# Linear attention and a mixer MLP on one core: loads over two queues, and the key sum z spread by crossbar turns

## The chip, the cores and the metric

The kernel runs on one core of a Trainium2 chip. The metric is device time in microseconds (us) of one execution; lower is better. A core has TensorE (PE, matmuls into PSUM), VectorE (DVE), ScalarE (ACT), GpSimd (POOL) and SyncE (SP, here only a queue that issues DMAs). ScalarE and GpSimd can issue DMAs as well.

## The reference

Two branches read the same `x` (2048 tokens of 640 channels, bf16) and are mixed by a gate per token. `B_x` is not used.

```python
qkv = x @ wqkv                                   # 640 -> 3*640, 32 heads of 20
pq, pk = phi(q), phi(k)                          # phi(t) = t+1 if t>0 else exp(t), + 1e-6
kv  = einsum("bhsd,bhse->bhde", pk, v)
z   = einsum("bhsd->bhd", pk)                    # sum of pk over all tokens: 640 numbers
num = einsum("bhqd,bhde->bhqe", pq, kv)
den = einsum("bhqd,bhd->bhq", pq, z) + 1e-6
a = (num / den) @ wo
h = gelu(layernorm(x) @ w1)                      # then four groups of channels are shifted by 1 or 2 tokens
x1 = x + shifted(h) @ w2
b = x1 + gelu(layernorm(x1) @ w3) @ w4
out = g * a + (1 - g) * b                        # g = sigmoid(sum(x * gate_w))
```

## The kernel before

The tokens lie in 16 tiles of 128 (tokens on the partitions), in four chunks of 512. Everything stays in SBUF. The stages overlap, but TensorE runs through them in about this order:

1. Head. TensorE first runs matmuls of ones (`warmup`, L854), then turns the first three x tiles itself (`t_x`, L763: five 128x128 transposes into one PSUM bank, then a VectorE copy into `xT`). `stream` (L873) with the order written out in `q_three` (L896) multiplies these tiles by the five 128-row blocks of wq, block by block as they land; `k_two` (L905) does the same for two k tiles. Each of these 25 steps is one matmul of 512 and one of 128 or 130 columns.
2. q and k tiles 2 to 15 (`k_tile`, `q_tile`). The x tiles from 3 on are turned by the DMA crossbar (`x_turn`, a transposing DMA on SP's queue). `phi` takes each result through ScalarE (Exp) and VectorE.
3. G = x-transposed times pk, in five row blocks (`gt_step`, L812) and a tail. ScalarE copies each finished block from PSUM into `GT`; the last block is item `("g", 4)`. On VectorE, 15 additions (`z_add`, L822) sum the 16 pk tiles to `zsum` (128 partitions of 640 partial sums).
4. `kvt_group` (L953; its matmuls are L969) multiplies wv by `GT`; VectorE masks the result into `Lt` (`lt_evac`), and two `m_step`s (L998) multiply it by wo into `M_sb`.
5. Around stage 4, `w1_group` (L1041) and `w2_tile` (L1049) of the MLP. They read `xnT`, the turned normalized x: GpSimd normalizes a tile into `xn` (a ring of three slots, `normalize`, L843), and SP issues its crossbar turn into `xnT` (`t_xn`, L849). ScalarE writes w1's results as `hsT`.
6. `zb_group` (L1025): two matmuls with a matrix of ones sum `zsum` over the partitions and spread the result over all of them; VectorE casts it to `zb`. `qn_sum` (L1086) multiplies each q tile by `zb` for the denominators.
7. w3, w4, the attention output (`a_tile`) and the mix.

Each engine runs its own instruction list in order. The order of the lists is not written out by hand but planned when the program is built: every piece of work is an item in a stream with dependencies and lags, and `_Items.run` always takes the item that a cost model expects to be ready first. An item puts all its instructions at the end of their engines' lists at once. The semaphore waits are derived from the buffers that instructions share. Loads go out in the order of the code:

```python
    for c in range(1, NCH):
        t0 = 5 if c == 1 else 4 * c
        dma_in(x_tok[:, t0:4 * c + 4, :], ...)
        for t in range(4 * c, 4 * c + 4):
            x_turn(t)
```

After the sixteen xn turns SP issues the loads of w3 and w4.

Of the kernel before, what the change touches and what calls it, by code (L numbers as in the profile page):

```python
# [6 lines left out]
F32 = mybir.dt.float32  # L7
ACTF = mybir.ActivationFunctionType
ALU = mybir.AluOpType
# [407 lines left out]
def _build(nc, A_x, A_wqkv, A_wo, B_w1, B_w2, B_w3, B_w4, gate_w, out, dbg=None, stop=None):  # L417
# [45 lines left out]
    def psb(b, n0, n1):  # L463
        return ps[:, b, :].bitcast(BF16)[:, n0:n1]
# [21 lines left out]
    M_sb = pa.alloc("M_sb", [128, KD, D], BF16)  # L486
    zb = pa.alloc("zb", [128, D], BF16)
    dnr = pa.alloc("dnr", [128, 2, 4, H], F32)
    xn = pa.alloc("xn", [128, 3, D], BF16)
    junk = pa.alloc("junk", [128, 1, D], BF16)  # L490
    qprod = pa.alloc("qprod", [128, D], F32)
# [22 lines left out]
    def bank():  # L514
        best = None
        for k_ in range(nbanks[0]):
            b = (bank_rr[0] + k_) % nbanks[0]
            if b in bank_pend or b in bank_hold:
                continue
            lk = sch.locks.get(b)  # L520
            tfree = 0.0 if lk is None else sch.ev_time.get((lk[1].sem, lk[1].val), 1e18)
            if best is None or tfree < best[0]:
                best = (tfree, b)
        bank_rr[0] = best[1] + 1
        bank_pend.add(best[1])
        return best[1]
# [4 lines left out]
    def pair():  # L531
        best = None
        for k_ in range(4):
            q_ = (bank_rr[0] // 2 + k_) % 4
            tf = 0.0
            ok = True
            for b in (2 * q_, 2 * q_ + 1):
                if b in bank_pend or b in bank_hold:
                    ok = False
                lk = sch.locks.get(b)  # L540
                if lk is not None:
                    tf = max(tf, sch.ev_time.get((lk[1].sem, lk[1].val), 1e18))
            if ok and (best is None or tf < best[0]):
                best = (tf, 2 * q_)
        b = best[1]
        bank_rr[0] = b + 2
        bank_pend.update((b, b + 1))
        return b
# [24 lines left out]
    def dve(fn, reads, writes, cost=None):  # L573
        if cost is None:
            n = nfree(writes[0])
            cost = 65.0 + n / 0.96
        return sch.op("dve", fn, reads, writes, cost=cost)
# [16 lines left out]
    def mm_group(out_ap, pairs, reads_extra=()):  # L594
        n = len(pairs)

        def fn(e, out_ap=out_ap, pairs=pairs, n=n):
            ins = None
            for i, (l, r) in enumerate(pairs):
                ins = e.matmul(out_ap, l, r, start=(i == 0), stop=(i == n - 1))  # L600
            return ins
        reads = [a for p in pairs for a in p] + list(reads_extra)
        return pe(fn, reads, [out_ap], cost=n * (max(nfree(pairs[0][1]), 24) * 0.4167 + 2.5))

    def tr_group(b, srcs):
        outs = [psb(b, 128 * i, 128 * (i + 1)) for i in range(len(srcs))]

        def fn(e, outs=outs, srcs=srcs):
            ins = None
            for o, s_ in zip(outs, srcs):  # L610
                ins = e.transpose(o, s_, ident[:])  # L611
            return ins
        return pe(fn, list(srcs) + [ident[:]], [psb(b, 0, 128 * len(srcs))], cost=len(srcs) * 56.0)
# [29 lines left out]
    def activation(out_ap, in_ap, func, scale=1.0, bias=0.0, accum=None):  # L643
        rd = [in_ap] + [a for a in (scale, bias) if not isinstance(a, (int, float))]
        wr = [out_ap] + ([accum] if accum is not None else [])
        n = nfree(out_ap)
        cost = max(150.0, 100.0 + 0.833 * n + (70.0 if in_psum(in_ap) else 0.0)) + 45.0 * (len(rd) - 1)
        if accum is not None:
            cost += 91.0
        st_ = ACT_SET.get(func)  # L650
        if st_ is not None and st_ != sch.act_func:
            cost += 1290.0
            sch.act_func = st_
        if accum is not None:
            return act(lambda e: e.activation(out_ap, in_ap, func, bias=bias, scale=scale, accum_out=accum), rd, wr, cost=cost)  # L655
        return act(lambda e: e.activation(out_ap, in_ap, func, bias=bias, scale=scale), rd, wr, cost=cost)  # L656
# [4 lines left out]
    def copy(engf, out_ap, in_ap):  # L661
        cost = None
        if engf is dve and in_ap.dtype == BF16 and out_ap.dtype == BF16:
            cost = 65.0 + nfree(out_ap) / 1.92
        return engf(lambda e: e.tensor_copy(out_ap, in_ap), [in_ap], [out_ap], cost=cost)  # L665
# [7 lines left out]
    def dma_in(out_ap, in_ap, key, **kw):  # L673
        return sch.dma("sp", out_ap, in_ap, key, **kw)

    sch.dma("act", junk[0:16, 0, 0:80].rearrange("p (k f) -> p k f", k=KD),
            A_wqkv[:, 0:16].rearrange("(k e r) f -> e r k f", k=KD, r=8)[:, 0, :, :], "touch")
    dma_in(x_tok[:, 0, :], x2[0:128, :], "x0")
    dma_in(x_tok[:, 1, :], x2[128:256, :], "x1")
    def load_wq(k):  # L680
        dma_in(wq[:, k, :], A_wqkv[128 * k:128 * (k + 1), 0:D], "wq%d" % k)

    load_wq(0)
    dma_in(x_tok[:, 2, :], x2[256:384, :], "x2")
    for k in range(1, KD):
        load_wq(k)
    for k in range(KD):
        dma_in(wkg[:, k, 0:D], A_wqkv[128 * k:128 * (k + 1), D:2 * D], "wk%d" % k)
        if k == 0:
            dma_in(x_tok[:, 3, :], x2[384:512, :], "x3")  # L690

    def x_turn(t):
        sch.dma("sp", xT[:, :, 128 * t:128 * (t + 1)], x_tok[:, t, :], "trx%d" % (t % 4), transpose=True)

    dma_in(x_tok[:, 4, :], x2[512:640, :], "x4")
    x_turn(3)
    gwr = xn[:, 1, 0:128]
    dve(lambda e: e.memset(gwr, 0.0), [], [gwr])
    sch.dma("act", xn[0:KD, 1, 0:128], gate_w.rearrange("(k p) -> k p", p=128), "gw")
    for c in range(1, NCH):  # L700
        t0 = 5 if c == 1 else 4 * c
        dma_in(x_tok[:, t0:4 * c + 4, :], x2[128 * t0:512 * (c + 1), :].rearrange("(n p) d -> p n d", p=128), "xc%d" % c)
# [54 lines left out]
        assert tags.get((buf, sl)) == what, ("stale ring slot", buf, sl, what, tags.get((buf, sl)))  # L757

    IT = _Items()
    WARM = 3200  # L760
    WARM2 = 512

    def t_x(t):  # L763
        b = bank()
        tr_group(b, [x_tok[:, t, 128 * k:128 * (k + 1)] for k in range(KD)])
        src = psb(b, 0, D).rearrange("p (k c) -> p k c", k=KD)
        dst = xT[:, :, 128 * t:128 * (t + 1)]
        if t == 2:
            mm_group(ps[:, b, 448:448 + KD], [(gwr, ident[:, 0:KD])])
        copy(dve, dst, src)  # L770
        if t == 2:
            copy(dve, wkg[:, :, D + 1:D + 2], ps[:, b, 448:448 + KD].rearrange("p (k o) -> p k o", o=1))

    def phi(b, dst, after_exp=None):
        se = slot("E", 3)
# [96 lines left out]

    def stream(order, w, n2, done):  # L873
        bs = {}
        for t, k in order:
            if k is None:
                if t is None:
                    warmup(256, 0.42)
                else:
                    t_x(t)  # L880
                continue
            if k == 0:
                bs[t] = pair()
                bank_hold.update((bs[t], bs[t] + 1))
            b = bs[t]
            l = xT[:, k, 128 * t:128 * (t + 1)]

            def fn(e, l=l, b=b, k=k):
                e.matmul(ps[:, b, 0:512], l, w[:, k, 0:512], start=(k == 0), stop=(k == KD - 1))  # L889
                return e.matmul(ps[:, b + 1, 0:n2], l, w[:, k, 512:512 + n2], start=(k == 0), stop=(k == KD - 1))  # L890
            pe(fn, [w[:, k, 0:512 + n2], l], [ps[:, b, 0:512], ps[:, b + 1, 0:n2]], cost=272.0)
            if k == KD - 1:
                bank_hold.difference_update((b, b + 1))
                done(t, b)

    def q_three():  # L896
        order = [(0, 0), (None, None), (1, 0), (2, None), (0, 1), (1, 1), (2, 0), (0, 2), (1, 2), (2, 1), (0, 3), (0, 4),
                 (1, 3), (2, 2), (1, 4), (2, 3), (2, 4)]
        stream(order, wq, 128, lambda t, b: phi(b, pq_tok[:, t + 1, :]))

    def k_out(t, b):
# [6 lines left out]
    def addA(name, dur, fn, deps=()):  # L908
        IT.add("A", name, dur, fn, deps)

    addA(("warm",), 0.0, lambda: warmup(WARM, 0.834))
    for i in range(2):
        addA(("tx", i), 0.28, lambda i=i: t_x(i))
    addA(("warm", 1), 0.0, lambda: warmup(WARM2, 0.42))
    addA(("q", 2), 4.08, q_three)
    addA(("k", 1), 2.72, k_two)
# [105 lines left out]
        for j in range(KD):  # L1022
            sch.dma("sp", M_sb[60:68, j, :], Mt[8 * j:8 * j + 8, :], "mt", group_total=KD)

    def zb_group():  # L1025
        b = pair()
        mm_group(ps[:, b, 0:512], [(ones_c[:, 0:128], zsum[:, 0:512])])
        mm_group(ps[:, b + 1, 0:128], [(ones_c[:, 0:128], zsum[:, 512:D])])
        copy(dve, zb[:, :], psf[:, 512 * b:512 * b + D])

    IT.add("KVF", ("kvt", 1), 0.0, kvt_group, deps=[(("g", KD - 1), 1.0)])
    IT.add("KVF", ("lt", 1), 0.0, lt_evac, deps=[(("kvt", 1), 0.0)])
    IT.add("KVF", ("m", 0), 0.0, m_last, deps=[(("lt", 1), 1.0), (("w1", 2, 2), 0.0)])
    IT.add("KVF", ("m", 1), 0.0, m_first, deps=[(("lt", 1), 1.0), (("w3", 0, 5), 0.0)])
    IT.add("MT", ("mt",), 0.0, m_tail, deps=[(("m", 1), 1.5), (("qt", 2), 0.0)])
    IT.add("ZB", ("zb",), 0.0, zb_group, deps=[(("z", NT - 1), 1.7), (("w2", 0), 0.0)])

    SHIFT = (1, -1, 2, -2)
    PIECES = [[(0, 128, SHIFT[j])] for j in range(4)] + [[(32 * g_, 32 * (g_ + 1), SHIFT[g_]) for g_ in range(4)]]
# [288 lines left out]
```

## Time and profile before

| | |
|---|---|
| time, median of 3 runs (lowest, highest) | 260.26 us (260.16, 260.85) |
| span of the profiled execution | 259.1 us |
| granted TensorE clock | 1.0 |
| w3 load, w4 load (SP) | 2160 KB, 9.3 us and 2080 KB, 14.8 us to landing |
| loads of one x, wq or wk block (SP) | 160 KB, 3.0, 3.9 and 4.1 us to landing |
| xnT turns (SP) | 32, 2.6 us to landing |

A page of the profile shows for each engine its busy time and share of the span, and for groups of equal instructions their line in the code, their number and mean length. A timeline line gives the start and the length in us, the engine, the line, the operation, and what it writes and reads; `x5` means five such instructions in a row, and a bracket at the end names how long the engine was idle before and what ended that. PEld is TensorE's loading of weights, which runs beside its matmuls; SPq, ACTq and POOLq are DMA issues on those queues. Many instructions come from small helpers, so one line (L600 for most matmuls, L656 for most activations) covers several tiles: the tile names tell them apart. Matmuls are pipelined, and their ends in the trace are modelled.

### The profile page before, as it was taken

How to read it: one execution, taken by the hardware profiler on the slowest of the kernel's cores; microseconds unless marked ns; L12 is line 12 of the kernel's file. 1: busy time of each engine (PE TensorE's matmuls, PEld its weight loads, DVE VectorE, ACT ScalarE, POOL GpSimd, SP SyncE). 2: the span in 40 equal slices, each digit the busy share in tenths (PEclk: the TensorE clock that was granted, in tenths of full speed). 3: DMA queues.
4: the chain of work that ended last, by engine and by line, in shares of the span. 5: the costliest groups of instructions: out<-in, count | busy, mean ns of one | idle time of the engine just before them, and what ended most of it. 6: DMA issues, size and time to landing. Idle time of an engine off the chain costs nothing.

```text
span 259.1 us, 4261 instructions
## 1 busy us (share of the span) xinstructions
PE 254.3 (98%) x1654; PEld 132.5 (51%) x1685; DVE 152.0 (59%) x288; ACT 106.6 (41%) x216; POOL 93.8 (36%) x151
## 2 busy tenths in 40 slices
PE   8999999999999999999999999999999999999996
PEld 4555555544454555554444445554455544455453
DVE  1587877899903799998997407992033410143233
ACT  1496677751365766676854240005500045100000
POOL 4013995969954029666914202320011110021001
DMA  6865998672856992552726640232000020000211
GB/s 181 246 148 137 155 226 156 186 121 50 99 109 124 355 338 47 62 101 52 105 53 122 124 66 0 47 90 67 0 3 0 3 101 0 0 3 1 104 51 51
DMA packets 51406, 25.16 MB, mean 97 GB/s; under 512 B 42766, under 2 KB 49975, under 8 KB 51386
## 3 DMA queue, kind: packets, MB, share of 16 engines
q1 hardware_dynamic: 50000, 21.47, 37.1%
q0 software_dynamic: 1136, 3.28, 5.1%
q8 instruction: 13, 0.21, 0.4%
q10 hardware_dynamic: 250, 0.14, 0.2%
q14 instruction: 7, 0.06, 0.1%
HBM read 12.05 MB, written 2.62 MB: 57 GB/s over the span
## 4 chain that ended last, share of the span: by engine, by line
PE 98%; issue 1%; DVE 1%
PE ps L600 61%; PE ps L1167 22%; PE ps L796 8%; PE ps L889 2%; PE ps L862 1%; PE ps L1079 1%; PE ps L1149 1%; PE ps L890 1%; PE ps L611 1%; DVE x_tok L639 0%; PE ps L969 0%; PE ps L998 0%; DVE xT L665 0%; PE ps L1146 0%
## 5 line engine op out<-in xcount | busy, mean ns | idle before, releaser
L600 PE MATMUL ps<-xnT,w 128*128 128x512 bf16 x348 | 80.4, 379 | 0.7 <-issue 0.2
L1167 PE MATMUL ps<-w,h2T 128*128 128x512 bf16 (+1 forms) x409 | 58.3, 298 | 0.5 <-issue 0.2
L656 ACT ACTIVATE h2T<-ps 128x512 bf16<-128x512 f32 x52 | 30.5, 598 | 67.5 <-PE ps L600 67.5
L600 PEld LDWEIGHTS ps<-xnT,w 128*128 128x128 bf16 x360 | 34.1, 98 | 38.5 <-issue 0.9
L639 DVE SCALAR_TENSOR_TENSOR x_tok<-ps,stg,abx 128x512 bf16<-128x512 f32 (+1 forms) x32 | 17.3, 550 | 61.5 <-PE ps L1167 61.5
L622 POOL TENSOR_SCALAR abx<-x_tok,stg 128x640 f32<-128x640 bf16 x16 | 15.3, 959 | 99.0 <-DVE x_tok L639 94.9
L1167 PEld LDWEIGHTS ps<-w,h2T 128*128 128x128 bf16 x416 | 32.1, 98 | 24.9 <-issue 1.1
L622 POOL TENSOR_SCALAR xn<-x_tok,st 128x640 bf16<-128x640 bf16 x32 | 35.0, 1102 | 14.4 <-DMA xnT<-xn 13.9
L656 ACT ACTIVATE Er<-ps 128x640 bf16<-128x640 f32 x32 | 22.4, 709 | 16.9 <-PE ps L600 8.4
L655 ACT ACTIVATE junk<-x_tok 128x640 bf16<-128x640 bf16 x32 | 23.6, 739 | 3.1 <-DVE x_tok L637 2.6
L656 ACT ACTIVATE hsT<-ps 128x512 bf16<-128x512 f32 (+1 forms) x32 | 18.9, 593 | 13.0 <-PE ps L600 12.7
L600 PE MATMUL ps<-M_sb,pqnT 128*128 128x128 bf16 (+1 forms) x156 | 23.6, 297 | 0.3
L600 PE MATMUL ps<-w,hsT 128*128 128x512 bf16 (+1 forms) x160 | 23.7, 299 | 0.0
L639 DVE SCALAR_TENSOR_TENSOR abx<-ps,stg,abx 128x640 f32<-128x640 f32 x16 | 14.1, 884 | 12.5 <-PE ps L600 11.5
L600 PE MATMUL ps<-wkg,xT 128*128 128x130 bf16 (+1 forms) x138 | 21.1, 298 | 0.1
L600 PE MATMUL ps<-wq,xT 128*128 128x128 bf16 (+1 forms) x128 | 19.7, 298 | 0.1
L600 PEld LDWEIGHTS ps<-w,hsT 128*128 128x128 bf16 x160 | 13.3, 98 | 12.1
L600 PEld LDWEIGHTS ps<-M_sb,pqnT 128*128 128x128 bf16 x160 | 13.2, 98 | 10.8
L796 PE MATMUL ps<-pk_tok,x_tok 128*128 128x512 bf16 x79 | 17.7, 379 | 0.1
L622 DVE TENSOR_SCALAR Er<-Er 128x640 bf16<-128x640 bf16 x32 | 11.8, 368 | 9.4 <-ACT Er L656 9.3
L637 DVE SCALAR_TENSOR_TENSOR x_tok<-ps,x_tok 128x640 bf16<-128x640 f32 x16 | 13.1, 820 | 6.8 <-PE ps L600 5.9
L1108 DVE TENSOR_TENSOR pq_tok<-pq_tok,dnr 128x300 bf16<-128x300 bf16 (+1 forms) x48 | 16.7, 401 | 0.6
(78 smaller groups left out, 228.0 us busy)
## 6 DMA issues: line engine op xcount, KB each, us to landing
w<-in_B_w_dram SPq DMA_DIRECT2D x1, 2160.0 KB, 9.3
w<-in_B_w_dram SPq DMA_DIRECT2D x1, 2080.0 KB, 14.8
out_dram<-x_tok SPq DMA_DIRECT2D x3, 640.0 KB, 3.1
x_tok<-in_A_x_dram SPq DMA_DIRECT2D x2, 640.0 KB, 5.5
w<-in_B_w_dram POOLq DMA_DIRECT2D x8, 160.0 KB, 4.5
x_tok<-in_A_x_dram SPq DMA_DIRECT2D x5, 160.0 KB, 3.0
wq<-in_A_wqkv_dram SPq DMA_DIRECT2D x5, 160.0 KB, 3.9
wkg<-in_A_wqkv_dram SPq DMA_DIRECT2D x5, 160.0 KB, 4.1
```

What stands on the lines that cost most here:

```text
L600: ins = e.matmul(out_ap, l, r, start=(i == 0), stop=(i == n - 1))
L611: ins = e.transpose(o, s_, ident[:])
L622: return engf(lambda e: e.tensor_scalar(out_ap, in_ap, s1, s2, op0, op1), rd, [out_ap], cost=cost)
L637: return dve(lambda e: e.scalar_tensor_tensor(out_ap, in0, scalar, in1, op0, op1, accum_out=accum), rd, [out_ap, accum], cost=cost + 70.0)
L639: return dve(lambda e: e.scalar_tensor_tensor(out_ap, in0, scalar, in1, op0, op1), rd, [out_ap], cost=cost)
L655: return act(lambda e: e.activation(out_ap, in_ap, func, bias=bias, scale=scale, accum_out=accum), rd, wr, cost=cost)
L656: return act(lambda e: e.activation(out_ap, in_ap, func, bias=bias, scale=scale), rd, wr, cost=cost)
L796: ins = e.matmul(o, l, r, start=(t0 + q_ == 0), stop=(t0 + q_ == NT - 1))
L862: ins = e.matmul(ps[:, b, 0:n], one[:, 0:128], one[:, 0:n], start=True, stop=True)
L889: e.matmul(ps[:, b, 0:512], l, w[:, k, 0:512], start=(k == 0), stop=(k == KD - 1))
L1108: dve(lambda e, o=o, i0=i0, i1=i1: e.tensor_tensor(o, i0, i1, ALU.mult), [i0, dnr[:, 1, sd, :]], [o], cost=cost)
L1167: ins = e.matmul(o, l, r, start=False, stop=(i == KFF - 1), skip_group_check=(n0 > 0))
```

## The change

The 160 KB loads of x, wq and wk, which all went out on SP's queue, are dealt out over SP's and ScalarE's queues. The small load of `gate_w` goes from ScalarE's queue to GpSimd's, and the tiny `touch` load on ScalarE's queue is dropped. The first warm-up has 3456 columns instead of 3200, the second 256 instead of 512. Tiles 0 and 1 of x are turned in two steps (block 0, then blocks 1 to 4) with a copy each, tile 1 inside `q_three`, whose order is new; `stream` takes its PSUM banks at the start.

`zb_group` is replaced by three items. `z_turn` turns `zsum` by the crossbar into the room of `zb`, so that channels lie on the partitions; `z_rows` sums over the free axis on VectorE (`zc`, five numbers in a partition) and has ScalarE copy them, repeated 128 times, back into the room of `zsum`; `z_back` turns that by the crossbar into `zb`. `z_turn` may be planned from item `("t1", 7)` on, the eighth xn turn. The two turns go to SP's queue.

```diff
-    sch.dma("act", junk[0:16, 0, 0:80].rearrange("p (k f) -> p k f", k=KD),
-            A_wqkv[:, 0:16].rearrange("(k e r) f -> e r k f", k=KD, r=8)[:, 0, :, :], "touch")
...
+    load_x(0)
+    load_wq(0, "act")
+    load_x(1)
+    load_wq(1, "act")
+    load_wq(2, "sp")
+    load_wq(3, "act")
+    load_x(2)
+    load_wq(4, "act")
+    load_wk(0, "sp")
+    load_wk(1, "act")
+    load_x(3)
+    load_wk(3, "act")
+    load_wk(2, "sp")
+    load_wk(4, "sp")
+    load_x(4)
+    x_turn(3)
+    sch.dma("pool", xn[0:KD, 1, 0:128], gate_w.rearrange("(k p) -> k p", p=128), "gw")
...
-    WARM = 3200
-    WARM2 = 512
+    WARM = 3456
+    WARM2 = 256
...
     def t_x(t):
+        for k0, k1 in ((0, 1), (1, KD)) if t < 2 else ((0, KD),):
+            b = bank()
+            tr_group(b, [x_tok[:, t, 128 * k:128 * (k + 1)] for k in range(k0, k1)])
...
+            copy(dve, xT[:, k0:k1, 128 * t:128 * (t + 1)], psb(b, 0, 128 * (k1 - k0)).rearrange("p (k c) -> p k c", k=k1 - k0))
...
     def q_three():
-        order = [(0, 0), (None, None), (1, 0), (2, None), (0, 1), (1, 1), (2, 0), (0, 2), (1, 2), (2, 1), (0, 3), (0, 4),
-                 (1, 3), (2, 2), (1, 4), (2, 3), (2, 4)]
+        order = [(0, 0), (1, None), (0, 1), (1, 0), (1, 1), (0, 2), (1, 2), (2, None), (0, 3), (1, 3), (0, 4), (2, 0),
+                 (2, 1), (1, 4), (2, 2), (2, 3), (2, 4)]
...
-    def zb_group():
-        b = pair()
-        mm_group(ps[:, b, 0:512], [(ones_c[:, 0:128], zsum[:, 0:512])])
-        mm_group(ps[:, b + 1, 0:128], [(ones_c[:, 0:128], zsum[:, 512:D])])
-        copy(dve, zb[:, :], psf[:, 512 * b:512 * b + D])
+    zT = zb[:, :].rearrange("p (k n) -> p k n", n=128)
+    zrep = zsum[:, :].rearrange("p (k n) -> p k n", n=128)
+
+    def z_turn():
+        sch.dma("sp", zT, zsum[:, :], "trz", transpose=True)
+
+    def z_rows():
+        dve(lambda e: e.tensor_reduce(zc[:, :], zT, mybir.AxisListType.X, ALU.add), [zT], [zc[:, :]], cost=820.0)
+        activation(zrep, zc[:, :].unsqueeze(2).to_broadcast([128, KD, 128]), ACTF.Copy)
+
+    def z_back():
+        sch.dma("sp", zT, zsum[:, :], "trz", transpose=True)
...
-    IT.add("ZB", ("zb",), 0.0, zb_group, deps=[(("z", NT - 1), 1.7), (("w2", 0), 0.0)])
+    IT.add("ZB", ("zt",), 0.0, z_turn, deps=[(("z", NT - 1), 1.7), (("t1", 7), 0.0)])
+    IT.add("ZB", ("zr",), 0.0, z_rows, deps=[(("zt",), 2.6)])
+    IT.add("ZB", ("zb",), 0.0, z_back, deps=[(("zr",), 1.5)])
```

More of the change, by code (lines that the diff above doesn't have):

```diff
@@ L488, in _build @@
     dnr = pa.alloc("dnr", [128, 2, 4, H], F32)
+    zc = pa.alloc("zc", [128, KD], F32)
     xn = pa.alloc("xn", [128, 3, D], BF16)
@@ L674, in dma_in, with load_x, load_wq, load_wk @@
         return sch.dma("sp", out_ap, in_ap, key, **kw)
-    sch.dma("act", junk[0:16, 0, 0:80].rearrange("p (k f) -> p k f", k=KD),
-            A_wqkv[:, 0:16].rearrange("(k e r) f -> e r k f", k=KD, r=8)[:, 0, :, :], "touch")
[L678 to L690, printed above, removed]
+    def load_x(t):
+        dma_in(x_tok[:, t, :], x2[128 * t:128 * (t + 1), :], "x%d" % t)
+    def load_wq(k, queue):
+        sch.dma(queue, wq[:, k, :], A_wqkv[128 * k:128 * (k + 1), 0:D], "wq%d" % k)
+    def load_wk(k, queue):
+        sch.dma(queue, wkg[:, k, 0:D], A_wqkv[128 * k:128 * (k + 1), D:2 * D], "wk%d" % k)
     def x_turn(t):
         sch.dma("sp", xT[:, :, 128 * t:128 * (t + 1)], x_tok[:, t, :], "trx%d" % (t % 4), transpose=True)
-    dma_in(x_tok[:, 4, :], x2[512:640, :], "x4")
-    x_turn(3)
     gwr = xn[:, 1, 0:128]
     dve(lambda e: e.memset(gwr, 0.0), [], [gwr])
-    sch.dma("act", xn[0:KD, 1, 0:128], gate_w.rearrange("(k p) -> k p", p=128), "gw")
+    load_x(0)
[15 more added lines that the diff above has]
+    sch.dma("pool", xn[0:KD, 1, 0:128], gate_w.rearrange("(k p) -> k p", p=128), "gw")
     for c in range(1, NCH):
@@ L759, in _build @@
     IT = _Items()
-    WARM = 3200
-    WARM2 = 512
+    WARM = 3456
+    WARM2 = 256
     def t_x(t):
[L764 to L772, printed above, removed]
+        for k0, k1 in ((0, 1), (1, KD)) if t < 2 else ((0, KD),):
+            b = bank()
+            tr_group(b, [x_tok[:, t, 128 * k:128 * (k + 1)] for k in range(k0, k1)])
+            if t == 2:
+                mm_group(ps[:, b, 448:448 + KD], [(gwr, ident[:, 0:KD])])
+            copy(dve, xT[:, k0:k1, 128 * t:128 * (t + 1)], psb(b, 0, 128 * (k1 - k0)).rearrange("p (k c) -> p k c", k=k1 - k0))
+            if t == 2:
+                copy(dve, wkg[:, :, D + 1:D + 2], ps[:, b, 448:448 + KD].rearrange("p (k o) -> p k o", o=1))
     def phi(b, dst, after_exp=None):
@@ L874, in stream @@
         bs = {}
+        for t in sorted({t for t, k in order if k is not None}):
+            bs[t] = pair()
+            bank_hold.update((bs[t], bs[t] + 1))
         for t, k in order:
@@ L881, in stream @@
                 continue
-            if k == 0:
-                bs[t] = pair()
-                bank_hold.update((bs[t], bs[t] + 1))
             b = bs[t]
@@ L911, in _build @@
     addA(("warm",), 0.0, lambda: warmup(WARM, 0.834))
-    for i in range(2):
-        addA(("tx", i), 0.28, lambda i=i: t_x(i))
+    addA(("tx", 0), 0.28, lambda: t_x(0))
     addA(("warm", 1), 0.0, lambda: warmup(WARM2, 0.42))
```

## The prediction

> **What bounds the kernel now.** I read the page first: TensorE is busy almost everywhere, and the chain that ended last is TensorE's too.
>
> ```profile
> PE 254.3 (98%) x1654; PEld 132.5 (51%) x1685; DVE 152.0 (59%) x288; ACT 106.6 (41%) x216; POOL 93.8 (36%) x151
> ...
> PE 98%; issue 1%; DVE 1%
> ```
>
> So a gain has to come out of TensorE's own instruction stream, and any wait put into that stream costs its full length, because nothing of 259.1 us is left to catch it up (4.8 us idle in all: 0.8 before the first matmul, over 2 at the tail). Two places are touched: the first 13 us, and the stretch from 70 to 86 us where z is finished and spread.
>
> For the head I read the weight loads of TensorE in the timeline. A bracket names the wait that ended just before:
>
> ```profile
> 3.34 1.11 PEld L611 LDWEIGHTS ps<-ident,x_tok 128*128 128x128 bf16 x10 [0.28 <-DMA x_tok<-in_A_x_dram]
> 4.88 0.10 PEld L889 LDWEIGHTS ps<-wq,xT 128*128 128x128 bf16 x1 [0.32 <-DMA wq<-in_A_wqkv_dram]
> 6.96 0.10 PEld L889 LDWEIGHTS ps<-wq,xT 128*128 128x128 bf16 x1 [0.38 <-DVE xT L665]
> ```
>
> The x tile lands at 3.34, wq's first block at 4.88, and one VectorE copy costs 0.38 more. The busy time by windows of 1 us from 2 to 10 shows the DMA engines at a mean share of 0.91 and 285 GB/s (mean of eight windows), from one queue.
>
> For the second place I put the timelines of the five engines side by side (columns: start, length, engine, line, what).
>
> ```profile
> 70.36 1.39 DVE L630 TENSOR_TENSOR zsum<-qprod,pk_tok 128x640 bf16<-128x640 f32 x1
> 77.72 0.95 DVE L630 TENSOR_TENSOR Lt<-ps,mask 128x120 bf16<-128x120 f32 x5 [5.97 <-PE ps L969]
> ```
>
> ```profile
> 74.50 0.60 ACT L656 ACTIVATE hsT<-ps 128x512 bf16<-128x512 f32 x1 [0.48 <-PE ps L600]
> 75.58 0.60 ACT L656 ACTIVATE GT<-ps 128x512 bf16<-128x512 f32 x1 [0.48 <-PE ps L796]
> ```
>
> ```profile
> 76.55 1.13 PE L969 MATMUL ps<-GT,wv 128*64 128x60 bf16 x55
> 83.30 0.43 PE L600 MATMUL ps<-zsum,ones_c 128*128 128x512 bf16 x2
> ```
>
> ```profile
> 73.77 1.20 SPq L281 DMA_TRANSPOSE xnT<-xn  x1
> 75.01 1.28 SPq L281 DMA_TRANSPOSE xnT<-xn  x1
> ```
>
> ```profile
> 72.87 1.74 POOL L622 TENSOR_SCALAR xn<-x_tok,st 128x640 bf16<-128x640 bf16 x2 [1.78 <-DMA xnT<-xn]
> 76.43 0.88 POOL L622 TENSOR_SCALAR xn<-x_tok,st 128x640 bf16<-128x640 bf16 x1 [0.59 <-DMA xnT<-xn]
> ```
>
> The reader is to see four things. zsum is complete at 71.75. The last copy of GT runs on ScalarE at 75.58 to 76.18, and TensorE's L969 group, which reads GT, starts at 76.55: a margin of 0.4 us. SP turns xn tiles one by one and is behind zsum: the tenth of the sixteen turns starts at 73.77, the eleventh at 75.01. And a turn takes 2.66 us from start to use (73.77 to GpSimd's resumption at 76.43, which waited for that turn's slot).
>
> **What the Trainium skill says.** "DMA: Bandwidth & Descriptors", Issuing engines are not separate DMA queues: loads issued from several engines end on the same 16 DMA engines and only issue time is saved. The trace agrees in that the engines are already 91% busy from one queue. "TensorE: Matmul & The Clock Gate", Architectural detail: ScalarE and VectorE run strictly in order, TensorE keeps its matmuls in order. The trace shows no instruction overtaking. The same page, The HAM clock gate: about 3.4 us of activity brings the full clock, and an idle window of about 3.4 us takes it away. The trace shows 512-column matmuls at 0.63 us until 5.2 and 0.38 from 5.63 on; it has no long idle stretch, so the second half is untested.
>
> **The change, part by part.**
>
> *z on TensorE.* Two matmuls (512 and 128 columns) and one VectorE cast of 0.82 go. By the chain, 512 + 128 columns cost 0.22 + 0.06 us; with rounding −0.27 on TensorE. The cast lies beside TensorE work and is worth nothing.
>
> *z on SP.* The program emits SP's turns as: ten xn turns (the one into GT stands between the second and the third), z's first turn, five xn turns, z's second turn, the last xn turn, then the w3 and w4 loads. So z's first turn takes the eleventh's place: issue at 75.01 although zsum is ready at 71.75, since it stands behind turns that wait for GpSimd's normalization. Landed and seen at 75.01 + 2.66 = 77.67.
>
> *z on VectorE.* The sum of 128x640 to 128x5 stands right behind zsum and ahead of the Lt multiplies. Its price is that of the TENSOR_REDUCE over 640 elements in the trace, 0.82: end at 78.49, +0.05 for the signal: 78.54. Lt would have started at 77.72 and is wanted only at 93.4 (L998), so VectorE hides this.
>
> *z on ScalarE.* This is the step that decides. In ScalarE's emitted stream the spreading copy (zsum from zc) stands between the fourth hsT evacuation (74.50) and the last GT copy (75.58). ScalarE then sits in front of it from about 75.1 until 78.54, and GT stands behind it. The copy is not in the trace; "ScalarE: Activation LUTs", What ACT_TABLE_LOAD costs, gives 186 ns + 0.833 ns per element and an overlap of 93 ns, so an estimate of 0.72 − 0.09 = 0.63 to the next start; the nearest row, the 128x640 Mt copy, has 0.71. GT starts at 79.17, ends at 79.77, and with 0.08 for the signal L969 starts at 79.85 instead of 76.55: TensorE stands still for **3.3 us**. Who waits behind: the whole TensorE stream (L969, then chunk 1 of w1, w2), and on ScalarE the four small hsT evacuations. These need 2.4 us from 79.8 to 82.2, while the first w2 group needs them at about 79.85 + 1.1 + 0.16 + 3×1.08 = 84.3: hidden. Bounds for the stall: sum of the unknown steps 0.4 us shorter (copy 0.45, reduce 0.6), or 0.4 longer: 2.9 to 3.7.
>
> *The other turns on SP.* The five xn turns after z's first move by 1.28, the last one and the w3 and w4 loads by two turns, about 2.5 us. The twelfth and the last turn, which end chunks 2 and 3, landed near 79 and 84.3, and w1 reached those chunks at 86.0 and near 97; w3 began to load at 82.95 with 9.3 us to landing and is first read after 100; TensorE itself is 3.3 us later. Nothing. z's second turn (about 82.8 to 85.4) serves the qs products, before at 85.88 and now later with TensorE: nothing.
>
> *The head.* Fifteen 160 KB loads go over two queues in another order, ScalarE issues six of 0.43 us (0.8 to 3.4; its first Exp was at 8.80: hidden), gate_w goes to GpSimd's queue (some 0.6 us ahead of the ones and identity tiles, which were done at 1.90 and are wanted at 3.3: hidden). The first x tile and wq's first block now come down together: 160 KB at 285 GB/s are 0.57 us, so x comes up to half a microsecond later (about 3.8) and wq0 about 1 us earlier (3.9). The warm-up grows by 256 columns of 0.83 ns, 0.21, and ends at 3.7. One transpose, its copy alone, then the first wq group at about 4.6 instead of 4.88. Until 5.6 the clock is halved in both, so what is left then counts: in both orders 24 of the 25 steps of 0.272 and one tile's transposes, 0.33, are left, 6.86, which gives 12.46. The first whole k tile began at 12.71, so 0.25 was wait. After, the wait is 0 to 0.5, for x's third tile, now seventh or eighth of the loads instead of fourth; I take 0.15. Value: **−0.1**; bounds −0.6 (the queues overlap better and more is done before 5.6) and +0.4.
>
> Sum on the profiled span: 3.3 − 0.27 − 0.1 = +2.93, from 259.1 to 262.0. The runs shown have the median at 260.26, 1.2 above that span: **263.2**.
>
> **Rivals.**
>
> *z's turn is early.* From issue to L969 the chain is 2.66 + 0.82 + 0.05 + 0.63 + 0.60 + 0.08 = 4.84 us; without a stall the issue must be at 76.55 − 4.84 = 71.7 or sooner, just when zsum is done. Then only the gains stay: −0.27 and −0.1 to −0.6, 259.4 to 259.9. It needs ten turns over by 71.7; they were at 75.0. Little speaks for it.
>
> *The turns are only partly late.* In the window 70 to 71 the DMA share reads 1.90 at 23 GB/s, and the turns issued at 68.27 and 69.69 land late (longest 4.5 us against 2.6). Without this dip the tenth turn would start near 72.2 and z's at 73.4: a stall of 1.7, and 261.6.
>
> *The clock falls.* A stop of 3.3 us is nearly the skill's idle window; half clock for another 3.4 us costs 1.7 more: 264.9.
>
> **How the numbers follow.** Main case 0.78 (own range 262.3 to 263.9); partly late 0.08; clock 0.07; early 0.07, of which half lies above and half below the bound of 0.3%, 0.8 us, which is about what a measurement of this kernel can tell from no change. Only the last is not slower: slower 0.93, same 0.03, faster 0.04. The range for 8 in 10 reaches a little into both neighbours: 262.0 to 264.4.
>
> **What would show it.** A gap of about 3.3 us on TensorE just before the L969 group (new number), put down to ScalarE's GT copy; that copy after the new zsum activation, itself after a TENSOR_REDUCE near 77.7; z's first turn starting near 75 with the SP queue full before it; no ones_c matmul at 83. The first whole k tile (L600, wkg), before at 12.71, would start within 0.5 us of that. I am wrong if GT's copy ends before 77, or if the gap sits elsewhere.

## The result, and the profile after

| | before | after |
|---|---|---|
| median (lowest to highest), runs taken side by side | 260.59 us (260.16 to 260.98, 6 runs) | 264.07 us (262.92 to 264.89, 6 runs) |
| span of the profiled execution | 259.1 us | 263.6 us |
| granted TensorE clock in it | 1.0 | 0.994 |

The ratio is 1.0131, with a 95% interval of 1.0099 to 1.0163. The six runs of after fall in two groups: two at clock 1.0 (262.92 and 263.18) and four at 0.994 (263.91 to 264.89). The profiled one is of the second group.

On the page of after, the engine line and the chain that ended last read:

```profile
PE 257.8 (98%) x1684; PEld 133.0 (50%) x1684; DVE 152.1 (58%) x290; ACT 107.4 (41%) x217; POOL 93.9 (36%) x152
...
PE 86%; POOL 6%; DMA 5%; ACT 1%; DVE 1%; SPq 1%; issue 0%
```

TensorE's busy share is still 98%, so this line alone would hide the loss. The chain doesn't: it was TensorE's for 98% of the span and is now TensorE's for 86%. Somewhere TensorE waited for a chain through GpSimd, SP's turns, VectorE and ScalarE. The chain of waits, in order of time (start, length, what), shows where. It leaves TensorE at 53.7 and comes back to it at 79.77:

```profile
50.97 2.74 PE ps L601 x20
53.73 0.70 ACT Er L657
54.50 0.72 ACT junk L656 x2
55.58 0.88 POOL st L631
...
73.65 0.88 POOL xn L623
...
74.90 2.63 DMA zb<-zsum
...
77.55 0.83 DVE zc L1038
...
78.41 0.73 ACT zsum L657
79.14 0.49 ACT GT L657
...
79.77 1.11 PE ps L975 x55
```

From 73.65 on these are the steps of the prediction, in its order. From the issue of z's turn to the kv group 4.87 us go by. The timelines of VectorE, ScalarE, TensorE, SP and GpSimd give the idle times with them:

```profile
70.91 1.38 DVE L631 TENSOR_TENSOR zsum<-qprod,pk_tok 128x640 bf16<-128x640 f32 x1
77.55 0.82 DVE L1038 TENSOR_REDUCE zc<-zb 128x5 f32<-128x640 bf16 x1 [5.26 <-DMA zb<-zsum]
```

```profile
75.05 0.60 ACT L657 ACTIVATE hsT<-ps 128x512 bf16<-128x512 f32 x1 [0.48 <-PE ps L601]
78.41 0.73 ACT L657 ACTIVATE zsum<-zc 128x640 bf16<-128x640 f32 x1 [2.76 <-DVE zc L1038]
79.05 0.58 ACT L657 ACTIVATE GT<-ps 128x512 bf16<-128x512 f32 x1
```

```profile
75.93 1.24 PE L601 MATMUL ps<-xnT,w 128*128 128x512 bf16 x5
79.77 1.11 PE L975 MATMUL ps<-GT,wv 128*64 128x60 bf16 x55 [2.60 <-ACT GT L657]
80.81 5.10 PE L601 MATMUL ps<-xnT,w 128*128 128x512 bf16 x15
```

```profile
67.39 7.46 SPq L281 DMA_TRANSPOSE xnT<-xn  x5
74.90 1.28 SPq L281 DMA_TRANSPOSE zb<-zsum  x1
76.22 6.57 SPq L281 DMA_TRANSPOSE xnT<-xn  x5
82.83 1.28 SPq L281 DMA_TRANSPOSE zb<-zsum  x1
```

```profile
72.75 1.77 POOL L623 TENSOR_SCALAR xn<-x_tok,st 128x640 bf16<-128x640 bf16 x2 [1.13 <-DMA xnT<-xn]
```

zsum is complete at 72.3, but SP issues its turn at 74.90, behind the xn turns (five of them in the row above it), which wait for GpSimd's normalization. ScalarE then stands 2.76 us for VectorE's five sums, and the GT copy, whose matmuls ended long before, stands behind the spreading copy. TensorE stands 2.60 us for GT.

The last TensorE line holds a second loss: fifteen matmuls in 5.10 us, 0.34 each, where the same fifteen at full clock need 0.23 (3.41 us in e5, below). The windows of 1 us (columns: busy time of PE, PEld, DVE, ACT, POOL with instructions, then PEclk, DMA share, GB/s) show why:

```profile
80.00:81.00 1.00, 1.00 (x53) 0.88 (x48) 0.08 (x1) 0.95 (x3) 0.73 (x1) 1.00 0.81 163
81.00:82.00 1.00, 1.00 (x4) 0.40 (x3) 0.84 (x5) 0.92 (x2) 0.54 (x2) 0.57 0.56 111
82.00:83.00 1.00, 1.00 (x3) 0.30 (x2) 0.00 (x0) 0.12 (x1) 0.48 (x1) 0.50 0.48 95
83.00:84.00 1.00, 1.00 (x4) 0.38 (x3) 0.00 (x0) 0.48 (x1) 0.00 (x0) 0.50 0.63 122
84.00:85.00 1.00, 1.00 (x5) 0.42 (x4) 0.00 (x0) 0.13 (x1) 0.00 (x0) 0.73 0.83 164
```

The granted clock (the third column from the right) falls to half some 4 us after TensorE stopped, when it is busy again. The missing clock adds up to 0.43 + 0.50 + 0.50 + 0.27 = 1.70 us.

The head, in the weight loads of TensorE and in its first whole k tile:

```profile
3.76 0.45 PEld L612 LDWEIGHTS ps<-ident,x_tok 128*128 128x128 bf16 x5 [0.16 <-DMA x_tok<-in_A_x_dram]
...
4.43 0.10 PEld L896 LDWEIGHTS ps<-wq,xT 128*128 128x128 bf16 x1
...
7.76 0.28 PEld L612 LDWEIGHTS ps<-ident,x_tok 128*128 128x128 bf16 x5 [0.78 <-DMA x_tok<-in_A_x_dram]
```

```profile
13.27 1.03 PE L601 MATMUL ps<-wkg,xT 128*128 128x512 bf16 x4
```

The first wq group starts 0.45 sooner, the third x tile is waited for 0.78, and the k tile starts 0.56 later than before. The difference of the spans, 4.5, is then 0.56 (head) + 2.60 (stop) + 1.70 (clock) − 0.27 (two matmuls gone) = 4.59, so nothing large is left over in this pair of traces.

### The profile page after: what moved, and what is told of

Its sections match the earlier page's. It is cut to its first block, busy times and chain, and to the rows that moved or that the text cites. A ratio compares the mean times of both kernels' runs of the same rounds, so it can differ in the third digit from the quotient of the medians.

```text
span 263.6 us, 4291 instructions
## 1 busy us (share of the span) xinstructions
PE 257.8 (98%) x1684; PEld 133.0 (50%) x1684; DVE 152.1 (58%) x290; ACT 107.4 (41%) x217; POOL 93.9 (36%) x152
## 4 chain that ended last, share of the span: by engine, by line
PE 86%; POOL 6%; DMA 5%; ACT 1%; DVE 1%; SPq 1%; issue 0%
PE ps L601 59%; PE ps L1182 21%; POOL xn L623 3%; DMA x_tok<-in_A_x_dram 2%; PE ps L896 2%; POOL st L631 2%; DMA xnT<-xn 1%; PE ps L803 1%; DMA zb<-zsum 1%; PE ps L1094 1%; PE ps L1164 1%; SPq L285 0%; PE ps L975 0%; PE ps L897 0%; DVE x_tok L640 0%
## 5 line engine op out<-in xcount | busy, mean ns | idle before, releaser
L601 PE MATMUL ps<-xnT,w 128*128 128x512 bf16 x360 | 83.2, 385 | 0.0
L601 PE MATMUL ps<-M_sb,pqnT 128*128 128x512 bf16 (+1 forms) x160 | 24.3, 299 | 0.0
L601 PE MATMUL ps<-wq,xT 128*128 128x512 bf16 (+1 forms) x130 | 19.8, 299 | 0.0
L1123 DVE TENSOR_TENSOR pq_tok<-pq_tok,dnr 128x300 bf16<-128x300 bf16 (+1 forms) x48 | 15.7, 381 | 0.6
```

What stands on the lines that cost most here:

```text
L1123: dve(lambda e, o=o, i0=i0, i1=i1: e.tensor_tensor(o, i0, i1, ALU.mult), [i0, dnr[:, 1, sd, :]], [o], cost=cost)
```

## The experiments

### One half of the change at a time

`e1_head_only` keeps the new loads and order of the head and puts back `zb_group` with its two matmuls. `e2_z_only` has the old head and the new z. Both are the parts of the diff shown above.

> The head of the change (loads over two queues, new order of the first steps, longer first warm-up) with the two ones matmuls for z kept. Theory A (ScalarE's order makes the loss, and the head adds a little): the first whole k tile starts 0.5 to 0.6 us later than the 12.71 of before, as in the changed kernel (13.27), no gap ahead of the kv group, time 0.4 to 0.7 us above before, 261.0 to 261.3. Theory B (the head is neutral and the difference in the trace of after is chance): within 0.2 us of before. Theory C (the head gains as it was written, and the z part loses more than was read): 0.3 us or more below before.

> The z part of the change alone, on the head of before. Theory A: z's first turn starts near 75.0, GT's last copy near 79.1, and the kv group waits 2.6 to 3.3 us; runs whose TensorE clock holds take 262.3 to 263.4, runs in which it is halved afterwards up to 1.8 us more. Theory D (the stall shrinks with an earlier head, since the wait has another cause such as the DMA load): under 261.

Head only: 260.74 us (260.27 to 261.88), ratio 1.0001 (0.9984 to 1.0018). z only: 264.71 (264.17 to 264.77), ratio 1.0144 (1.0123 to 1.0165). The head is neutral in the times, as the second of its expectations had it, and the whole loss that can be measured comes with z. In the trace of z alone TensorE stands 2.67 us, with its clock at 0.50 to 0.58 afterwards:

```profile
79.67 1.45 PE L970 MATMUL ps<-GT,wv 128*64 128x60 bf16 x55 [2.67 <-ACT GT L657]
```

In the trace of head only the k tile starts late too (13.48), and the times don't show it. That start varies from one execution to the next: in the traces of this study the old head gave 12.71, 13.02, 12.83 and 12.90 (mean 12.87), the new one 13.27, 13.48, 12.75, 12.70, 13.50, 13.55 and 13.57 (mean 13.26; the sixth is that of `e7_x2_step_later` below, which changes one more step of the head). So one pair of traces says little on it; the times bound the new head at −0.4 to +0.5 us.

### The spreading copy behind GT

`e3_copy_late` has after's head, `e4_z_only_copy_late` the old one. In both, `z_rows` may only be planned when w1's chunk 0 is through, which puts the copy behind the last GT copy in ScalarE's list (and the sum, which is part of the same item, behind the Lt multiplies on VectorE); the w3 load is kept behind z's second turn.

```diff
-    IT.add("ZB", ("zr",), 0.0, z_rows, deps=[(("zt",), 2.6)])
+    IT.add("ZB", ("zr",), 0.0, z_rows, deps=[(("zt",), 2.6), (("w1", 0, KD - 1), 0.0)])
-    IT.add("MISC", ("w3load",), 0.0, w3_load, deps=[(("k", NT - 1), 0.0), (("t1", NT - 1), 0.0)])
+    IT.add("MISC", ("w3load",), 0.0, w3_load, deps=[(("zb",), 0.0), (("k", NT - 1), 0.0), (("t1", NT - 1), 0.0)])
```

> The changed kernel, with only the place of the spreading copy in ScalarE's list moved: it comes after the last GT copy and the first chunk's hsT evacuations (and the w3 load after z's second turn, so that this turn isn't queued behind it). Both turns, the sum and the copy stay. Theory A (the order on ScalarE is the cause): no gap ahead of the kv group, clock 1.0, and what is left is the head's +0.56 and the two matmuls' -0.27: 260.7 to 261.1, 3 us below the changed kernel. Theory E (the two turns themselves cost, by pushing the xn turns and the w3 and w4 loads back on SP, or by loading the DMA engines): the loss stays over 1.5 us, with TensorE waiting for xnT or w3 instead.

> The head of before, and z by turns with the copy placed after GT's last copy, as in the run before this one. Theory A: TensorE's stream is that of before without the two ones matmuls, and nothing else waits: 0.1 to 0.3 us below before. If the qs products wait for the later z (its second turn lands near 85.5, where before they began at 85.88), VectorE holds up the w2 evacuations and it is slower than before by some tenths.

After with the late copy: 261.05 us (260.1 to 265.98), ratio 1.0017 (1.0005 to 1.003); with the old head 260.92 (260.43 to 263.01), ratio 1.0012 (0.9998 to 1.0026). The lines of ScalarE and TensorE in e3:

```profile
75.62 0.60 ACT L657 ACTIVATE GT<-ps 128x512 bf16<-128x512 f32 x1 [0.48 <-PE ps L803]
80.52 0.73 ACT L657 ACTIVATE zsum<-zc 128x640 bf16<-128x640 f32 x1
```

```profile
76.59 1.14 PE L975 MATMUL ps<-GT,wv 128*64 128x60 bf16 x55
```

z's first turn was still issued as late as 74.34, but with GT ahead of it the stop is gone, and so is the fall of the clock. So the late turn makes a stop only with the copy ahead of GT in ScalarE's list. (One of e3's 22 runs, the one at 265.98, has a clock of 0.994 and isn't in the ratio; there is no trace of it, and it stays unexplained.) In e4, which was expected a little below before, the second turn goes out at 83.80, VectorE gets z late and falls behind, and TensorE waits for it twice, 0.25 us at 93.98 and 0.27 us at 113.65: together about twice what the two removed matmuls were to bring.

### Keeping TensorE busy through the stop

`e5_filler` is after with ten matmuls of ones ahead of the kv group, into the PSUM bank that this group then overwrites. They add work that the result doesn't use.

```diff
+        def fill(e):
+            ins = None
+            for _ in range(10):
+                ins = e.matmul(ps[:, b, :], one[:, 0:128], one, start=True, stop=True)
+            return ins
+        pe(fill, [], [ps[:, b, :]], cost=0.0)
         pe(fn, [wvf[:, :], GT[:, :, :]], [ps[:, b, 0:360]], cost=1000.0)
```

> The changed kernel, with ten matmuls of ones (512 columns, 2.2 us) put on TensorE ahead of the kv group, into the PSUM bank that this group then overwrites: it is busy where it stood still. They take nothing away, since GT's copy still comes near 79.1. Theory A with the clock (an idle stretch of 2.6 us can halve the granted clock for some 3 us): the kv group still starts near 79.8, the clock reads 1.0 all along, and the time is 262.6 to 263.2, at the level of those runs of the changed kernel whose clock held (262.92 and 263.18), 1 us below its median. Theory F (the slow matmuls after the gap have another cause, or the stall alone makes the whole 3.5 us): the same 264 as the changed kernel.

It took 262.91 us (262.37 to 263.63), ratio 1.0088 (1.0066 to 1.011), all five runs at clock 1.0. The lines of TensorE:

```profile
76.44 2.35 PE L982 MATMUL ps<-const-bfloat16-1.0 128*128 128x512 bf16 x10
79.26 1.11 PE L975 MATMUL ps<-GT,wv 128*64 128x60 bf16 x55 [0.47 <-ACT GT L657]
80.30 3.41 PE L601 MATMUL ps<-xnT,w 128*128 128x512 bf16 x15
```

The kv group still waits for GT, only busy instead of idle, and the fifteen matmuls behind it now need 3.41 us instead of 5.10: 1.69 less, the 1.70 counted above. In the times the gain is 1.2 us on after's median, and nothing on after's two runs at full clock. The stop thus cost more than its length, and the second part is the clock.

### z's turns earlier on SP

`e6_turn_early` is after with z's first turn two places ahead in SP's list; `e9_both_turns_early` also has the second one three places ahead (the fourth and fifth line of the diff are in e9 alone).

```diff
+        sp = sch.prog["sp"]
+        i = [sem for (_, _, sem) in sp].index("d:trz")
+        sp.insert(i - 2, sp.pop(i))
+        i = [sem for (_, _, sem) in sp].index("d:trz", i)
+        sp.insert(i - 3, sp.pop(i))
         sch.emit()
```

> The changed kernel with one entry of SP's list moved: z's first turn stands before the ninth xn turn, two places further ahead. ScalarE's list is that of the changed kernel, so the spreading copy still stands ahead of the last GT copy. Theory A (GT comes late by as much as the turn stands late in SP's queue): the turn is issued near 72.2 in place of 74.9, the kv group starts 4.87 us after it, at 77.1, when TensorE is free for it anyway: a gap under 0.4 us, clock 1.0, 260.3 to 261.1. Theory G (the copy ahead of GT costs wherever the turn stands, or the turn is bound by zsum or the DMA engines and not by its place): a gap of over 1.5 us stays.

> As the run with z's first turn two places ahead on SP (262.55 us), and its second turn also three places ahead. In that run the second turn was issued at 83.89 although the spread sums were ready at 77.55; z's row reached VectorE at 86.55, its q products started behind it, and TensorE stood 1.41 us at 96.63 for a PSUM bank that VectorE had not yet emptied. Theory A (the rest of that run's loss is the second turn standing behind w1's turns on SP): issued by 80.1, z lands by 82.8, VectorE starts its first q product when its other operands are there, the stop of 1.41 us goes, and the time is 261.2 (260.7 to 261.8), with what is left to the head. Theory B (two crossbar turns among the xn turns cost TensorE elsewhere, whatever their place): it stays at 262.2 to 262.9, with a new wait of TensorE for one of the three xn turns that z's second turn now stands before.

e6: 262.55 us (261.79 to 263.1), ratio 1.007 (1.005 to 1.009). The turn went out at 73.40, GT was copied at 77.46, the kv group started at 78.18 with no wait ahead of it, and the clock held: the stop was gone, and still half the loss stayed, against an expectation of 260.3 to 261.1. The trace is that of the slowest of the six runs, and some of its loss need not be z's: its k tile starts at 13.50, and TensorE waits 0.66 us at 45.88 for a tile of x that the crossbar turned late, before z is touched. The chain of waits has this as

```profile
38.05 7.79 DMA xT<-x_tok
...
45.88 2.89 PE ps L604 x20
```

The largest wait comes behind z, read from SP's, VectorE's and TensorE's timelines:

```profile
83.89 1.28 SPq L281 DMA_TRANSPOSE zb<-zsum  x1
```

```profile
86.55 0.82 DVE L634 TENSOR_TENSOR qprod<-pq_tok,zb 128x640 f32<-128x640 bf16 x1 [1.67 <-DMA zb<-zsum]
...
95.75 0.81 DVE L641 SCALAR_TENSOR_TENSOR x_tok<-ps,x_tok 128x640 bf16<-128x640 f32 x1
```

```profile
96.63 1.25 PE L604 MATMUL ps<-xnT,w 128*128 128x512 bf16 x5 [1.41 <-DVE x_tok L641]
```

The spread sums were ready at 77.55, but their turn was issued at 83.89. VectorE stood 1.67 us for z, then worked with no wait that the timeline shows until 96.56, and emptied the PSUM bank that TensorE wanted 1.41 too late. In e9 that turn has the earlier place:

```profile
79.16 1.27 SPq L281 DMA_TRANSPOSE zb<-zsum  x1
```

```profile
84.03 0.82 DVE L636 TENSOR_TENSOR qprod<-pq_tok,zb 128x640 f32<-128x640 bf16 x1
```

```profile
94.40 1.25 PE L606 MATMUL ps<-xnT,w 128*128 128x512 bf16 x5
```

The q product no longer waits for z, TensorE no longer waits for VectorE, and the time is 260.74 us (259.53 to 261.57), ratio 1.0011 (1.0001 to 1.0021): 1.8 below e6 and 3.3 below after, with the same instructions. (This run's head waits 0.8 for x all the same. The wait for a turned x tile that e6 had at 45.88 isn't in this trace, so a part of the difference of the two traces is chance; the medians, over 6 and 22 runs, are what counts.) The xn turns that z's turns now stand before cost nothing that the trace shows.

### The head's third tile, and the best version of z

`e7_x2_step_later` is e1 with the third x tile turned two steps later, so that TensorE doesn't stand in front of its load.

```diff
-        order = [(0, 0), (1, None), (0, 1), (1, 0), (1, 1), (0, 2), (1, 2), (2, None), (0, 3), (1, 3), (0, 4), (2, 0),
+        order = [(0, 0), (1, None), (0, 1), (1, 0), (1, 1), (0, 2), (1, 2), (0, 3), (1, 3), (2, None), (0, 4), (2, 0),
```

> The run with the head alone, with the transposes of the third x tile two steps later in TensorE's order (after the fourth wq block of tiles 0 and 1). In the changed kernel and with the head alone TensorE waited 0.5 to 0.8 us for that tile. If that wait is where the gain of the earlier start went, the first whole k tile starts 0.3 to 0.6 us sooner than with the head alone (13.0 or less), and the time is 0.2 to 0.5 us below it. If the loads as a whole bound the head, the wait only moves to wq's last blocks and nothing changes.

261.19 us (260.52 to 262.17), ratio 1.0027 (1.0018 to 1.0035): no gain, and if anything a loss against head only (1.0001). The wait only moved, to 0.40 for a wq block at 7.01 and 0.65 for the tile's copy at 9.16, and the k tile started at 13.55. That fits the second expectation, that the loads as a whole set the head's end and not the step that happens to stand in front of one of them; no run changed the loads alone, so it isn't shown. The hoped-for gain of 0.2 to 0.5 us did not come.

`e8_z_both_early` is the old head with both turns early and the copy behind GT.

```diff
-        IT.add("T1", ("t1", u), 0.0, lambda u=u: t_xn(1, u), deps=[(("n1", u), 1.1)])
+        IT.add("T1", ("t1", u), 0.0, lambda u=u: t_xn(1, u), deps=[(("n1", u), 1.1)] + ([(("zt",), 0.0)] if u == 8 else [(("zb",), 0.0)] if u == 14 else []))
-    IT.add("ZB", ("zr",), 0.0, z_rows, deps=[(("zt",), 2.6)])
+    IT.add("ZB", ("zr",), 0.0, z_rows, deps=[(("zt",), 2.6), (("g", KD - 1), 0.0)])
```

> The head of before, z's first turn before the ninth xn turn, the copy behind GT's last copy and the first chunk's hsT evacuations, and z's second turn before the last two xn turns, so that it isn't behind w3's load. In the two runs with the late copy the second turn landed 3.9 us after its issue, next to w3's load, and the qs products held up two w2 evacuations by 0.25 us each. Theory: with zb ready by 84.5 that is gone, and TensorE has only two matmuls less: 0.1 to 0.4 us below before. If it is at before's level or above, the two matmuls were worth nothing that can be measured, or another wait took their place.

260.62 us (260.16 to 261.14), ratio 1.0002 (0.9991 to 1.0012). The 0.1 to 0.4 us below before that were expected aren't there. With no stop of TensorE left behind the head in its trace, the new z is worth nothing that can be measured; no version here beats the kernel before.

## Why the prediction was right, and where its terms were off

The forecast was 263.2 us in a range of 262.0 to 264.4; the median is 264.07. The likeliest case took place in its steps on SP, VectorE and ScalarE, and the rival of the falling clock came on top of it in four runs of six. That the median still lies within the range is in part luck: the stop was taken 0.7 us too long, and the clock, left out of the sum, cost 1.70 where it fell. The two errors go against each other; the forecast stop together with the fall would have given the 264.9 of that rival, above the range.

- *z on SP.* Predicted: issue at 75.01, in the eleventh turn's place. Measured 74.90, landed and seen 2.65 later (2.66 predicted). The place is right, and e9 shows that the places of the two turns in SP's list make the difference of 3.3 us. That the time fits to 0.1 is luck, as the size of the stop shows.
- *VectorE.* Its 0.82 for the sum is exact.
- *z on ScalarE, the decisive step.* The copy took 0.73 from start to end and 0.64 to the next start. The estimates from the Trainium skill, "ScalarE: Activation LUTs", What ACT_TABLE_LOAD costs, were 0.72 and 0.63: this trace agrees. From issue to kv group 4.87 us, 4.84 predicted; the group started at 79.77, 79.85 predicted. e3 shows that it was the order in ScalarE's list, as the step said.
- *The size of the stop.* Predicted 3.3, measured 2.60, below its lower bound of 2.9. The steps from the issue on are right to 0.03 together; what was off is how long after TensorE's own work the turn is issued. The eleventh place was read at 75.01 in the trace of before, 62.30 behind the start of the first whole k tile (12.71). In after it is 74.90 − 13.27 = 61.63, and in e2, e3, e4 and e5 61.68, 61.59, 61.73 and 61.67; in e1, which has the old z, the eleventh turn comes at 74.97 − 13.48 = 61.49. The trace of before was the odd one: GpSimd stood 1.78 us for a turn's slot before it resumed at 72.87, and 0.91 to 1.22 us at that place in all ten other traces, e1 and e7 among them (the line of e1 stands below this list). So the turn came 0.67 sooner against TensorE, which is the miss of 0.7. In the absolute time this was hidden, since the head of the profiled run was 0.56 late and delayed GpSimd's chain as well: that chain leaves TensorE only at 53.7. The stop hardly depends on the head: 2.67 in e2, whose k tile starts at 13.02.
- *The head.* Predicted −0.1 within −0.6 to +0.4; in the trace +0.56, outside the bounds and 0.06 beyond the "within 0.5" of the last paragraph; in the times (e1) 0.0. The named place was right, the wait for x's third tile, and its size wrong: 0.15 taken, 0.78 measured at the weight loads. One trace can't price this head to better than about 0.4.
- *The clock.* Given a chance of 0.07 and a price of 1.7. The price is what the trace has, 1.70. The chance was far too small. I took the Trainium skill's idle window ("TensorE: Matmul & The Clock Gate", The HAM clock gate, about 3.4 us) as a bound that a stop of 3.3 would hardly reach. The runs differ from the page: in after, with a stop of 2.60 in the profiled run, the clock fell in four runs of six, and in e2, with 2.67, in four of five. All of e5's 5 and of e9's 22 runs held it. With the stop as measured and the head at the 0.0 of e1's times, 260.59 + 2.60 − 0.27 = 262.92 without a fall, and 1.70 more, 264.62, with one; the two runs at full clock have 263.05 on average, the four others 264.48.
- *z's second turn: "nothing".* True in after, only because TensorE itself was late: the first q product starts at 88.06, while the turn was issued at 82.83. Without the stop the place of this turn costs up to 1.41 us (e6). This term was right by the cover of the other.
- *−0.27 for the two matmuls.* In the traces without a stop, the span less the shift of the k tile differs from before by −0.34 (e3: 258.8 with +0.04), −0.36 (e9: 259.6 with +0.86) and −0.09 (e8: 259.2 with +0.19); in e4 (259.7 with +0.12), less its two waits of 0.52, by −0.04. The sign is that of the term, the times show no gain, and it stays open at this size.
- *Rival "the turns are only partly late".* It came true in part, without being seen as such: in the chain of after the turn issued at 68.81 takes 3.85 us, in before the one issued at 68.27, at the same distance from the k tile, 4.5. This is where the 0.7 of the stop went. What makes the dip was not tried.

The line of e1 for the size of the stop; that of before, with 1.78, stands in the prediction:

```profile
72.82 1.73 POOL L622 TENSOR_SCALAR xn<-x_tok,st 128x640 bf16<-128x640 bf16 x2 [0.98 <-DMA xnT<-xn]
```

## What to carry to other kernels

When work is moved from a busy engine to idle ones, look at the lists it is put into: what stands behind it on each engine and queue, and who waits for that. Here the same instructions cost 3.5 us more than before or 0.3 us by the places of two turns on SP, and a copy of 0.7 us cost a multiple of itself by standing in front of another. A stop of the engine that sets the time must be priced with the clock that may fall after it; and when one stop is taken away, look for the wait that it had covered. A time read off a single trace carries that execution's accidents: measure it from the work that it hangs on, and compare more than one trace where there are some.

## What was not expected of the hardware

The granted clock fell to half after an idle stretch of only 2.60 us, and it fell late: the first window with a lower clock is at 81 to 82, when TensorE had been busy again for over 1 us; it came back between 84 and 85. In e2 the window 80 to 81 is the first one, at 0.58, while the kv group had started at 79.67: sooner after the restart than in after. Within one kernel it fell in some runs and not in others (four of six). In e6, whose trace has a stop of 1.41, it held in all six runs.
